# Moving one transposition ahead of its product, and the conversions around it, in a delta-rule attention with a gated MLP

## The chip, the cores and the metric

The kernel runs on one core of one Trainium2 chip. The metric is device microseconds of one execution. TensorE (PE) multiplies, VectorE (DVE) and ScalarE (ACT) do the elementwise work, GpSimd (POOL) clears a few buffers, SyncE (SP) issues the DMAs. Each engine runs its own list of instructions in order, and waits at an instruction until what it reads has been written and what it overwrites has been read.

## The reference

For each of 4 batches and 8 heads there is a recurrence over 768 tokens with a 48 x 48 state; its outputs, 3072 tokens of 384 numbers, go through a gated MLP of width 1536.

```python
k_n = k / (norm(k) + 1e-6)
for t in range(S):
    y[t] = q[t] @ state
    v_old = k_n[t] @ state
    state = state + beta[t] * outer(k_n[t], v[t] - v_old)
x = y.transpose(0, 2, 1, 3).reshape(B * S, H * D)
out = (sigmoid(x @ w_gate) * (x @ w_val)) @ w_out
```

## The kernel before

**Groups.** The tokens are cut into 12 groups of 64 per sequence (N = 12). Within a group the recurrence is solved as a triangular system: `gram` forms the products of keys (`G`, `L`), `norms` the key norms from them, a solver the inverse of the unit triangular matrix in blocks of 32, `rest`, `updates` and `rows` apply it to V and to the state, `advance` brings the state to the next group, and `flip` transposes the result into the MLP's input. Groups 0, 1 and 2 use `solve_halves`: it inverts 16-wide halves on DVE in `H`, copies them into `X` (L397), transposes `X` into `mt` (L400), and then joins the halves. The joining takes a product `pz` of `mt` with a lower-left block (L407, on PE), a second transposition `D` of `mt` on DVE (L420), a copy `Z` of `pz` on ACT (L421; `D` and `Z` lie in the tile `scratch`), a second product `pm` of both (L407), and the subtraction of `pm` from `mt` (L428). Groups 3 to 11 use `solve`, which has no joining.

**The MLP.** For each group the MLP runs in 12 pieces f of the hidden width: `gate_val` (PE, tile `gv`), `gated` (sigmoid on ACT at L564, product on DVE at L565, tile `sg`) and `outp` (PE, tile `po`) two pieces later. Group 0 multiplies full fp32 weights `u` (L556, L584); groups 1 to 11 multiply weights and inputs split into a high and a low part (`w`, L559, L590), the split on ACT (L212, high part) and DVE (L219, low part).

**Weights.** 36 pieces are loaded as 64-bit words (`raw`). ACT converts each piece in two instructions (`scaled`, L189 and L191), and the end of the conversion of piece n releases the load of piece n + 6. DVE joins the two words of a piece (L203, `u`). Later each `u` is split.

**Order.** The order on every engine is written by hand: `plan`, `late` and `tail` hold, for each slot s, steps that are issued in that slot. A slot pair issues one `gate_val` and one `outp`; `plan[s]` comes before the gating work of the slot, `late[s]` behind it, `tail[s]` last. Generators (`halves1`, `splits`, `scalings`) are advanced by the count that stands in the tables, from one `yield` to the next. So the place of a `yield` decides what is issued together. In `solve_halves` the transposition L400 and the product `pz` stand between the same two `yield`s, so for group 1 both are issued in slot 10, and for group 2 in slot 29.

`scale_v` multiplies V of a group by the key norms, 16 small ACT instructions (L279); `R`, the difference of V and `pk` (L455), needs it. PSUM tiles come from pools of two buffers; `pz` and `pm` take the two `aux` buffers that the key products of group 2 (`pg_2`) used before, and `pp_1` (keys by queries, L319) takes them next.

Of the kernel before, what the change touches and what calls it, by code (L numbers as in the profile page):

```python
# [55 lines left out]
def deltanet_gated_mlp(ctx: ExitStack, tc: tile.TileContext, kd, qd, kv, beta, words, out):  # L56
# [106 lines left out]
    pieces = [(0, "g"), (0, "v")]  # L163
# [20 lines left out]
    def scaled(n):  # L184

        half, lo, hi = words_of(n)
        nc.scalar.activation(lo.bitcast(I32), half, AF.Copy, bias=-4095.5 / 8192, scale=1 / 8192)  # L189
        h = hi.bitcast(F32)  # L190
        done[n] = nc.scalar.activation(h, h, AF.Prelu, scale=2.0 ** -112, alpha=-2.0 ** 32)  # L191
        if n + BEHIND in range(EAGER, len(pieces)):
            load_piece(n + BEHIND, done[n])
# [27 lines left out]
    def joining():  # L221
        for n in range(len(pieces)):
            join(n)
            yield

    def splitting():
        for n in range(len(pieces) + 1):
            if n:
                weight_lo(n - 1)
            if n < len(pieces):  # L230
                weight_hi(n)
            yield
# [43 lines left out]
    def scale_v(g):  # L276
        V, mq = state[g]["kv"][:, 1], state[g]["mq"]
        for c in range(CP):
            nc.scalar.activation(V[:, c], V[:, c], AF.Copy, scale=mq[:, c, 0:1])  # L279
            yield  # L280
# [92 lines left out]
    def solve_halves(g):  # L373
# [14 lines left out]
        for j in range(15, 0, -1):  # L388
            k, n = j // 2, 8 - j // 2
# [8 lines left out]
            yield  # L398
        A, D, Z = (joints[g][:, i] for i in range(3))
        nc.vector.transpose(mt.rearrange("q c (k r) -> q k c r", r=2), X.rearrange("q k (c r) -> q k c r", r=2))  # L400
        pool, tag = (ps_aux, "aux") if g else (ps_gv, "gv")
        pz, pm = (pool.tile([128, CP, 32], F32, name=f"{n}_{g}", tag=tag) for n in ("pz", "pm"))

# [199 lines left out]
    plan = collections.defaultdict(list)  # L603
    late = collections.defaultdict(list)

    def steps(gen, n=1):
        def fn():
            for _ in range(n):
                next(gen, None)
        return fn  # L610

    def spread(gen, total, lo, hi, room=lambda s: 1.0, into=plan):

        done, upto, whole = 0, 0.0, sum(room(s) for s in range(lo, hi))
        for s in range(lo, hi):
            upto += total * room(s) / whole
            n = total if s == hi - 1 else round(upto)
            into[s].append(steps(gen, n - done))
            done = n

    def chain(*gens):
        for q in gens:
            yield from q

    def take(gen, n=1):
        for _ in range(n):
            next(gen, None)

    def scaling(g, s):
        for i in range(4):  # L630
            plan[s + i].append(steps(scalings[g], 4))

    scalings = [scale_v(g) for g in range(N)]
    NORMS, SOLVE, HALVES = 18, 66, 40
    joins, splits = joining(), splitting()
# [27 lines left out]
    take(gram(1), 10)  # L663
    take(scale_v(0), CP)
    halves0, norms1, halves1 = solve_halves(0), norms(1), solve_halves(1)
    take(halves0, 38)
    for n in range(2, 6):
        scaled(n)
    take(norms1, 11)
# [28 lines left out]
    flip(0, 1)  # L698
    busy_array(gap[0], 2)
    tail = collections.defaultdict(list)  # L700
    for n, at in enumerate((0, 0, 0, 1, 2, 2, 4, 5, 6, 8, 9, 10, 11, 12, 12, 13, 14, 15, 16, 16, 17, 18, 18), 13):
        plan[at].append(lambda n=n: scaled(n))
    spread(joins, len(pieces) - 4, 0, 20)
    for at, n in ((0, 8), (1, 4), (2, 6), (3, 4), (4, 5), (5, 5), (9, 1), (10, 1), (11, 1)):
        plan[at].append(steps(halves1, n))
    plan[10].append(steps(halves1))
    spread(splits, 12, 9, 24, into=tail)
    spread(splits, len(pieces) + 1 - 12, 24, 44, into=tail)
    for s in (7, 8):
        plan[s].append(steps(scalings[1], 8))  # L710
    for part in (1, 0):
        plan[6].append(lambda part=part: load_rows(2, part))
    plan[8].append(lambda: load_q(2))
    halves2 = solve_halves(2)
    plan[12].append(lambda: clear(2))
    plan[23].append(lambda: joint(2))
    plan[24].append(lambda: lower_left(2))

    busy = collections.Counter()
# [18 lines left out]
    for g in range(N):  # L738
# [20 lines left out]
        else:  # L759
# [4 lines left out]
            if g > 2:  # L764
                solves.append((g, w - 13 if g == 3 else w - 14, w + 9))
            scaling(g, {2: 25, 3: 43}.get(g, w - 7))
    spread(chain(norms(2), halves2), NORMS + 36, 8, 27, lambda s: max(0.1, 1.6 - busy[s]))
    for at in (29, 30, 30, 31):
        plan[at].append(steps(halves2))
    for g, lo, hi in solves:  # L770
        spread(chain(norms(g), solve(g)), NORMS + SOLVE, lo, hi, lambda s: max(0.1, 1.6 - busy[s]))
# [72 lines left out]
```

## Time and profile before

| what | value |
|---|---|
| time, median of 3 runs | 651.9 us (651.75 to 652.64) |
| the profiled execution's own time | 652.21 us |
| its span, first to last instruction | 650.5 us |
| mean granted TensorE clock | 0.991 |
| PE busy | 626.4 us (96%) |
| DVE busy | 467.9 us (72%) |
| ACT busy | 321.2 us (49%) |

The profiled execution takes 1.7 us around its span and stands 0.3 us above the median. Times in the text are microseconds from the start of the span. In a list of instructions by time, the first number is the start, the second the time until the end of the (merged) instructions of that row, "x" their count, and in brackets the idle time of the engine ahead of them and what ended it. In the table by stretches each engine's busy time is followed by its number of instructions; PEclk is the granted TensorE clock as a share of full speed.

### The profile page before, as it was taken

How to read it: one execution, taken by the hardware profiler on the slowest of the kernel's cores; microseconds unless marked ns; L12 is line 12 of the kernel's file. 1: busy time of each engine (PE TensorE's matmuls, PEld its weight loads, DVE VectorE, ACT ScalarE, POOL GpSimd, SP SyncE). 2: the span in 40 equal slices, each digit the busy share in tenths (PEclk: the TensorE clock that was granted, in tenths of full speed). 3: DMA queues.
4: the chain of work that ended last, by engine and by line, in shares of the span. 5: the costliest groups of instructions: out<-in, count | busy, mean ns of one | idle time of the engine just before them, and what ended most of it. 6: DMA issues, size and time to landing. Idle time of an engine off the chain costs nothing.

```text
span 650.5 us, 24072 instructions
## 1 busy us (share of the span) xinstructions
PE 626.4 (96%) x10556; PEld 585.0 (90%) x10556; DVE 467.9 (72%) x1443; ACT 321.2 (49%) x870; POOL 11.3 (2%) x30
## 2 busy tenths in 40 slices
PE   6788999799999999999999999999999999999996
PEld 4466778789999999999999999999999999999996
DVE  5887687568887977977967977977977977952221
ACT  5889385566455355355355355355355355334221
POOL 5000000000000000000000000000000000000000
PEclk9999799899999999999999999999999999999999
DMA  9597422201212103112102012113112100100101
GB/s 256 193 323 249 131 75 84 51 4 32 77 28 85 25 28 85 25 28 84 25 28 85 20 33 84 26 28 85 25 28 84 25 4 3 25 3 3 25 1 25
DMA packets 17769, 41.07 MB, mean 63 GB/s; under 512 B 4224, under 2 KB 7296, under 8 KB 17664
## 3 DMA queue, kind: packets, MB, share of 16 engines
q1 hardware_dynamic: 17664, 39.53, 21.1%
q8 instruction: 83, 1.36, 0.9%
q14 instruction: 22, 0.18, 0.1%
HBM read 34.80 MB, written 4.72 MB: 61 GB/s over the span
## 4 chain that ended last, share of the span: by engine, by line
PE 89%; DVE 5%; ACT 3%; issue 1%; DMA 1%; ACTq 0%; SPq 0%; DVEq 0%
PE gv L559 43%; PE po L590 22%; PE gv L556 4%; PE pu L475 3%; PE pg L291 2%; PE yy L501 2%; PE yy L504 2%; PE pp L319 2%; PE po L584 2%; PE pd L522 2%; PE pk L444 1%; PE pk L467 1%; PE pt L540 1%; ACT kv L279 1%; DVE kqp L324 1%
## 5 line engine op out<-in xcount | busy, mean ns | idle before, releaser
L559 PE MATMUL gv<-xx,w 128*128 128x256 f32 x2376 | 308.5, 284 | 0.0
L559 PEld LDWEIGHTS gv<-xx,w 128*128 128x128 f32 x2376 | 302.3, 191 | 0.9
L590 PE MATMUL po<-w,h 128*128 128x384 f32 x792 | 166.5, 345 | 0.0
L564 ACT ACTIVATE sg<-gv 128x256 f32<-128x256 f32 x144 | 55.3, 384 | 203.4 <-PE gv L559 190.6
L590 PEld LDWEIGHTS po<-w,h 128*128 128x128 f32 x792 | 133.3, 188 | 3.4 <-issue 0.3
L565 DVE TENSOR_TENSOR sg<-sg,gv 128x256 f32<-128x256 f32 x144 | 60.4, 419 | 85.2 <-ACT sg L564 84.7
L570 ACT CAST h<-sg 128x256 fp32r<-128x256 f32 x132 | 53.5, 405 | 53.0 <-DVE sg L565 51.6
L350 DVE TENSOR_TENSOR X<-X,tmp 128x126 f32<-128x126 f32 (+22 forms) x279 | 71.3, 256 | 8.9
L347 DVE TENSOR_TENSOR tmp<-X,gp 128x126 f32<-128x126 f32 (+22 forms) x279 | 71.0, 254 | 7.9
L575 DVE TENSOR_TENSOR h<-sg,h 128x256 fp32r<-128x256 f32 x132 | 55.1, 417 | 29.8 <-ACT h L570 29.8
L481 ACT COPY su<-pu 32x384 f32<-32x384 f32 x92 | 43.3, 471 | 15.2 <-PE pu L475 14.0
L279 ACT ACTIVATE kv<-kv,mq 128x48 f32<-128x48 f32 x192 | 48.1, 329 | 0.0
L556 PE MATMUL gv<-xx,u 128*128 128x256 f32 x144 | 35.8, 402 | 0.3 <-DVE xx L543 0.3
L529 DVE TENSOR_TENSOR su<-su,pd 48x384 f32<-48x384 f32 x40 | 22.1, 552 | 18.9 <-PE pd L522 18.4
L324 DVE TENSOR_TENSOR kqp<-pp,pmask 64x512 f32<-64x512 f32 x48 | 32.3, 687 | 3.4 <-PE pp L319 2.4
L303 ACT COPY G<-pg 32x256 f32<-32x256 f32 (+1 forms) x69 | 25.4, 368 | 18.6 <-PE pg L291 17.4
L556 PEld LDWEIGHTS gv<-xx,u 128*128 128x128 f32 x144 | 28.2, 201 | 5.5 <-ACT xx L543 0.8
L455 DVE TENSOR_TENSOR R<-kv,pk 128x384 f32<-128x384 f32 x44 | 22.4, 550 | 1.5 <-PE pk L444 1.5
L212 ACT CAST w<-u 128x384 fp32r<-128x384 f32 x36 | 18.2, 508 | 6.2 <-DVE w L219 5.9
L475 PEld LDWEIGHTS pu<-R,mt 32*32 32x32 f32 x1408 | 16.5, 105 | 4.9 <-issue 1.7
L219 DVE TENSOR_TENSOR w<-u,w 128x384 fp32r<-128x384 f32 x36 | 19.4, 550 | 1.5 <-ACT w L212 1.4
L475 PE MATMUL pu<-R,mt 32*32 32x48 f32 x1408 | 19.4, 202 | 0.9 <-DVE kqp L324 0.9
(104 smaller groups left out, 518.3 us busy)
## 6 DMA issues: line engine op xcount, KB each, us to landing
raw<-in_words_dram SPq DMA_DIRECT2D x36, 384.0 KB, 5.0
kv<-in_kv_dram SPq DMA_DIRECT2D x24, 384.0 KB, 5.0
kqp<-in_qd_dram SPq DMA_DIRECT2D x24, 256.0 KB, 4.2
kqp<-in_kd_dram SPq DMA_DIRECT2D x24, 192.0 KB, 3.6
out_dram<-ot SPq DMA_DIRECT2D x48, 96.0 KB, 2.2
beta<-in_beta_dram SPq DMA_DIRECT2D x12, 16.0 KB, 4.5
```

Of the source, the lines that this page charges most:

```text
L279: nc.scalar.activation(V[:, c], V[:, c], AF.Copy, scale=mq[:, c, 0:1])
L347: nc.vector.tensor_tensor(out=tmp, in0=X[:, k:16, j:j + 1].to_broadcast([128, n, j]), in1=gp[:, j:j + 1, 0:j].to_broadcast([128, n, j]), o ...
L350: nc.vector.tensor_tensor(out=X[:, k:16, 0:j], in0=X[:, k:16, 0:j], in1=tmp, op=ALU.add)
L475: nc.tensor.matmul(out=pu[0 if g else x][r:r + 32, j], lhsT=mt[r:r + 32, e * J + j], rhs=R[e][r:r + 32, j], start=True, stop=True)
L481: nc.scalar.copy(su[r:r + 32, 3 if x else e], pu[0][r:r + 32])
L556: nc.tensor.matmul(out=pg[:, o], lhsT=parts[w, f][:, k * 128:(k + 1) * 128], rhs=x[0][:, k], start=k == 0, stop=k == KC - 1)
L559: nc.tensor.matmul(out=pg[:, o], lhsT=parts[w, f][:, a, k * 128:(k + 1) * 128], rhs=x[b][:, k], start=(k == 0 and q == 0), stop=(k == KC - ...
L564: nc.scalar.activation(h, st["gv", f][:, 0], AF.Sigmoid)
L565: nc.vector.tensor_tensor(out=h, in0=h, in1=st["gv", f][:, 1], op=ALU.mult)
L570: nc.scalar.copy(hh[:, 0], st["sg", f])
L575: nc.vector.tensor_tensor(out=hh[:, 1], in0=st["sg", f], in1=hh[:, 0].bitcast(F32), op=ALU.subtract)
L590: nc.tensor.matmul(out=po[s], lhsT=hh[:, a, ts], rhs=parts["o", f][:, w], start=(f == 0 and q == 0), stop=(f == NF - 1 and q == 2))
```

## The change

A `yield` now stands between the transposition L400 and the product `pz`, so the tables can issue the transposition in an earlier slot than the product. The other edits follow from that or go with it:

- `take(halves0, 39)`: group 0 takes one step more, since it has one `yield` more; its order is the same as before.
- Group 1: the transposition is issued in slot 6 (the added `(6, 1)`), the product stays in slot 10.
- Group 2: the steps of norms and halves are spread over slots 8 to 24 instead of 8 to 26, the transposition is issued in slot 26, the product stays in slot 29.
- Conversions of pieces 15 to 23 (`scaled`) are issued up to three slots later; piece 24 and those behind it stay, and so do 13 and 14.
- V of group 1 is scaled four instructions at a time at the end of slots 4 to 7, instead of eight at a time within slots 7 and 8.
- Splits of weights 12 to 30: three steps in slots 24 to 28, the others in slots 29 to 43; before, 25 steps were spread evenly over 24 to 43.

```diff
         A, D, Z = (joints[g][:, i] for i in range(3))
         nc.vector.transpose(mt.rearrange("q c (k r) -> q k c r", r=2), X.rearrange("q k (c r) -> q k c r", r=2))
+        yield
         pool, tag = (ps_aux, "aux") if g else (ps_gv, "gv")
...
-    take(halves0, 38)
+    take(halves0, 39)
...
-    for n, at in enumerate((0, 0, 0, 1, 2, 2, 4, 5, 6, 8, 9, 10, 11, 12, 12, 13, 14, 15, 16, 16, 17, 18, 18), 13):
+    for n, at in enumerate((0, 0, 1, 2, 3, 5, 6, 8, 9, 9, 10, 10, 11, 12, 12, 13, 14, 15, 16, 16, 17, 18, 18), 13):
         plan[at].append(lambda n=n: scaled(n))
     spread(joins, len(pieces) - 4, 0, 20)
-    for at, n in ((0, 8), (1, 4), (2, 6), (3, 4), (4, 5), (5, 5), (9, 1), (10, 1), (11, 1)):
+    for at, n in ((0, 8), (1, 4), (2, 6), (3, 4), (4, 5), (5, 5), (6, 1), (9, 1), (10, 1), (11, 1)):
         plan[at].append(steps(halves1, n))
     plan[10].append(steps(halves1))
     spread(splits, 12, 9, 24, into=tail)
-    spread(splits, len(pieces) + 1 - 12, 24, 44, into=tail)
-    for s in (7, 8):
-        plan[s].append(steps(scalings[1], 8))
+    spread(splits, 3, 24, 29, into=tail)
+    spread(splits, len(pieces) + 1 - 15, 29, 44, into=tail)
+    for s in range(4, 8):
+        tail[s].append(steps(scalings[1], 4))
...
-    spread(chain(norms(2), halves2), NORMS + 36, 8, 27, lambda s: max(0.1, 1.6 - busy[s]))
-    for at in (29, 30, 30, 31):
+    spread(chain(norms(2), halves2), NORMS + 36, 8, 25, lambda s: max(0.1, 1.6 - busy[s]))
+    for at in (26, 29, 30, 30, 31):
         plan[at].append(steps(halves2))
```

Lines behind the new `yield` are one higher in the changed kernel, and two higher from the loop over `scalings` on. The lists of PE and POOL are the same in both kernels. What moves stands on DVE, ACT and SP, at these places.

**DVE, group 1.** The list of DVE before, from the last join ahead of the sigmoid product of piece 3 (`u_7` from `raw_14`) to the transposition into `mt`:

```order
L203 SCALAR_TENSOR_TENSOR u_7_1013<-raw_14_620 128x384
L565 TENSOR_TENSOR sg_0_3_1024<-sg_0_3_1024,gv_0_3_1002 128x256
L203 SCALAR_TENSOR_TENSOR u_7_1013<-raw_15_716 128x384
L203 SCALAR_TENSOR_TENSOR u_8_1030<-raw_16_720 128x384
L203 SCALAR_TENSOR_TENSOR u_8_1030<-raw_17_772 128x384
L240 STREAM_TRANSPOSE gp_2_1062<-G_2_918 128x1024
L565 TENSOR_TENSOR sg_0_4_1064<-sg_0_4_1064,gv_0_4_1040 128x256
L455 TENSOR_TENSOR R_1_0_1101<-kv_1_113,pk_1_0_1067 128x384
L455 TENSOR_TENSOR R_1_1_1102<-kv_1_113,pk_1_1_1068 128x384
L203 SCALAR_TENSOR_TENSOR u_9_1111<-raw_18_776 128x384
L203 SCALAR_TENSOR_TENSOR u_9_1111<-raw_19_803 128x384
L400 STREAM_TRANSPOSE mt_78<-X_1_559 128x16x16x2
```

and in the changed kernel:

```order
L397 COPY X_1_559<-H_1_725 128x8x16 x2
L203 SCALAR_TENSOR_TENSOR u_7_1013<-raw_14_620 128x384
L400 STREAM_TRANSPOSE mt_78<-X_1_559 128x16x16x2
L566 TENSOR_TENSOR sg_0_3_1025<-sg_0_3_1025,gv_0_3_1002 128x256
L203 SCALAR_TENSOR_TENSOR u_7_1013<-raw_15_716 128x384
L203 SCALAR_TENSOR_TENSOR u_8_1035<-raw_16_720 128x384
L203 SCALAR_TENSOR_TENSOR u_8_1035<-raw_17_772 128x384
L240 STREAM_TRANSPOSE gp_2_1055<-G_2_914 128x1024
```

The transposition goes ahead of ten instructions; the others keep their order among themselves, and behind the joins of `u_9` follow at once the small instructions of `norms(2)`, the joins of `u_10` and the transposition `D`, as before.

**ACT, group 1.** The list of ACT before, from the sigmoid of piece 2 on (`raw` rows are conversions, `kv_1` the scaling of V, `G_2` and `L_2` copies of key products of group 2):

```order
L564 ACTIVATE sg_0_2_980<-gv_0_2_954 128x256
L189 ACTIVATE raw_20_807<-raw_20_807 128x384
L191 ACTIVATE raw_20_807<-raw_20_807 128x384
L303 COPY G_2_918<-pg_2_1_921 32x32x8 x2
L189 ACTIVATE raw_21_811<-raw_21_811 128x384
L191 ACTIVATE raw_21_811<-raw_21_811 128x384
L308 COPY L_2_919<-pg_2_0_920 32x256 x2
L308 COPY L_2_919<-pg_2_1_921 32x256 x2
L564 ACTIVATE sg_0_3_1024<-gv_0_3_1002 128x256
L279 ACTIVATE kv_1_113<-kv_1_113,mq_1_669 128x48 x8
L189 ACTIVATE raw_22_833<-raw_22_833 128x384
L191 ACTIVATE raw_22_833<-raw_22_833 128x384
```

and in the changed kernel:

```order
L565 ACTIVATE sg_0_2_972<-gv_0_2_950 128x256
L279 ACTIVATE kv_1_113<-kv_1_113,mq_1_669 128x48 x4
L189 ACTIVATE raw_18_776<-raw_18_776 128x384
L191 ACTIVATE raw_18_776<-raw_18_776 128x384
L303 COPY G_2_914<-pg_2_1_917 32x32x8 x2
L279 ACTIVATE kv_1_113<-kv_1_113,mq_1_669 128x48 x4
L189 ACTIVATE raw_19_803<-raw_19_803 128x384
L191 ACTIVATE raw_19_803<-raw_19_803 128x384
L308 COPY L_2_915<-pg_2_0_916 32x256 x2
L308 COPY L_2_915<-pg_2_1_917 32x256 x2
L565 ACTIVATE sg_0_3_1025<-gv_0_3_1002 128x256
L279 ACTIVATE kv_1_113<-kv_1_113,mq_1_669 128x48 x8
```

Before, the other eight scalings and then the sigmoid of piece 4 follow, then pieces 23, 24 and the copy `Z` (one weight split between). In the changed kernel there follow piece 20, the sigmoid of piece 4, then pieces 21 to 24 and the copy `Z`. Ahead of the sigmoid of piece 4 stand pieces up to 22 before, up to 20 now; the conversion of piece 18 was already ahead of the copies of the state (L527), and 19 behind them.

**DVE, group 2.** The list of DVE before, from the low part of the first hidden piece of group 1 (`h_1_0`) to the transposition:

```order
L575 TENSOR_TENSOR h_1_0_1798<-sg_1_0_1786,h_1_0_1798 128x256
L565 TENSOR_TENSOR sg_1_1_1866<-sg_1_1_1866,gv_1_1_1839 128x256
L219 TENSOR_TENSOR w_13_1837<-u_6_991,w_13_1837 128x384
L219 TENSOR_TENSOR w_14_1870<-u_7_1013,w_14_1870 128x384
L219 TENSOR_TENSOR w_15_1873<-u_7_1013,w_15_1873 128x384
L575 TENSOR_TENSOR h_1_1_1889<-sg_1_1_1866,h_1_1_1889 128x256
L565 TENSOR_TENSOR sg_1_2_1918<-sg_1_2_1918,gv_1_2_1894 128x256
L455 TENSOR_TENSOR R_2_0_1955<-kv_2_1015,pk_2_0_1921 128x384
L455 TENSOR_TENSOR R_2_1_1956<-kv_2_1015,pk_2_1_1922 128x384
L219 TENSOR_TENSOR w_16_1892<-u_8_1030,w_16_1892 128x384
L400 STREAM_TRANSPOSE mt_78<-X_2_1349 128x16x16x2
```

and in the changed kernel:

```order
L324 TENSOR_TENSOR kqp0_76<-pp_2_1_1802,pmask_81 64x512 x2
L400 STREAM_TRANSPOSE mt_78<-X_2_1349 128x16x16x2
L576 TENSOR_TENSOR h_1_0_1799<-sg_1_0_1787,h_1_0_1799 128x256
L566 TENSOR_TENSOR sg_1_1_1864<-sg_1_1_1864,gv_1_1_1837 128x256
L219 TENSOR_TENSOR w_12_1791<-u_6_987,w_12_1791 128x384
L576 TENSOR_TENSOR h_1_1_1884<-sg_1_1_1864,h_1_1_1884 128x256
L566 TENSOR_TENSOR sg_1_2_1910<-sg_1_2_1910,gv_1_2_1886 128x256
L456 TENSOR_TENSOR R_2_0_1947<-kv_2_1016,pk_2_0_1913 128x384
L456 TENSOR_TENSOR R_2_1_1948<-kv_2_1016,pk_2_1_1914 128x384
L219 TENSOR_TENSOR w_13_1868<-u_6_987,w_13_1868 128x384
L219 TENSOR_TENSOR w_14_1952<-u_7_1013,w_14_1952 128x384
L421 STREAM_TRANSPOSE scratch_2_1750<-mt_78 128x512
```

The transposition goes ahead of ten instructions, and three weight splits fewer stand ahead of `R_2` (12 is the last there, 15 before) and four fewer ahead of `D` (14 is the last, 18 before). On ACT the high parts of the same weights move back likewise: ahead of the sigmoid of `sg_1_2` 13 is the last now, 16 before. On SP the load of V and K rows of group 2 and one query load now stand ahead of the loads of pieces 26 to 28, which follow their conversions.

## The prediction

> **What bounds the kernel now.** I read the table by stretches first, to see where PE stops and where its clock drops; then the waits; then the chain of waits through the two stops. Columns of the table: stretch and length, then busy time of PE, weight loads, DVE, ACT and POOL, then PEclk, DMA share and GB/s.
>
> ```profile
> core 0: us, PE busy (x) PEld busy (x) DVE busy (x) ACT busy (x) POOL busy (x), PEclk, DMA share, GB/s
> 35.22:38.63 3.41, 2.19 (x65) 1.19 (x52) 2.33 (x8) 1.63 (x5) 0.00 (x0) 1.00 1.02 350
> ...
> 62.52:65.93 3.41, 0.70 (x3) 0.08 (x1) 2.46 (x6) 3.11 (x9) 0.00 (x0) 1.00 1.02 279
> 65.93:69.34 3.41, 2.81 (x130) 2.66 (x131) 3.27 (x10) 0.59 (x1) 0.52 (x1) 0.50 0.67 219
> 69.34:72.75 3.41, 3.41 (x9) 2.70 (x8) 0.68 (x4) 0.00 (x0) 0.00 (x0) 0.50 0.02 5
> ...
> 120.54:123.95 3.41, 0.38 (x44) 0.41 (x46) 2.96 (x7) 1.68 (x6) 0.00 (x0) 1.00 0.64 155
> 123.95:127.36 3.41, 3.41 (x116) 3.35 (x104) 1.31 (x3) 1.05 (x2) 0.00 (x0) 0.50 0.02 5
> ...
> 130.00:640.00 510.00, 508.84 (x8300) 496.23 (x8300) 370.55 (x1157) 231.18 (x643) 0.00 (x0) 1.00 0.14 36
> ```
>
> From 130 us on PE works 508.84 of 510 us, so what PE gains earlier comes out at the end, and nothing there can be gained by order. Before, there are two holes, and behind each the granted clock is 0.50: for 6.8 us behind the first, for 3.4 us behind the second. Who ends the holes:
>
> ```profile
> PE pz L407 <- DVE mt L400: 3.4, 1, 3.4
> PE pz L407 <- DVE n L244: 3.3, 1, 3.3
> ...
> PE pu L475 <- DVE kqp L324: 0.9, 1, 0.9
> ```
>
> Both large ones are the product `pz`. The second row names L244, the instruction right behind the transposition L400 on DVE; in the chain it is L400 itself that ends just ahead of `pz`:
>
> ```profile
> 65.76 0.62 DVE mt L400
> 66.53 1.93 PE pz L407 x128
> 68.46 4.93 PE gv L556 x12
> 73.39 1.22 PE pm L407 x82
> 76.09 1.09 PE pp L319 x64
> 77.18 2.79 PE gv L556 x12
> ...
> 123.58 1.75 PE pz L407 x81
> 125.33 3.27 PE gv L559 x18
> 128.60 1.22 PE pm L407 x82
> 131.07 2.16 PE gv L559 x18
> ```
>
> The same 12 matmuls of `gv` take 4.93 us behind the first hole and 2.79 us at 77.18; the same 18 take 3.27 us behind the second and 2.16 us at 131.07. PE was done with its last product ahead of the holes at these times (start plus length: 63.22 and 120.21; the first row ends the product that a sigmoid is to read below, at 52.90):
>
> ```profile
> 50.04 2.86 PE L556 MATMUL gv<-xx,u 128*128 128x256 f32 x12
> ...
> 61.66 1.56 PE L584 MATMUL po<-u,sg 128*128 128x384 f32 x4
> ...
> 118.89 1.32 PE L590 MATMUL po<-w,h 128*128 128x384 f32 x6
> ```
>
> **The change part by part.** PE's list does not change, so the question is only what each of its waits finds.
>
> *Group 1, the transposition.* `X` is complete well ahead of both holes (the join `u_7` behind its copies and the transposition now stand in front of the sigmoid product of piece 3), and the two PSUM buffers are read out by the copies of `pg_2` ahead of the sigmoid of piece 3, at 58.30 before. So `pz` follows its neighbour at 63.22, 3.31 us earlier, and takes 1.22 us (the row of `pm`, as many matmuls at full clock) in place of 1.93; the `gv` behind it takes 2.79 in place of 4.93. PE then stands before `pm` at 63.22 + 1.22 + 2.79 = 67.23, where it stood at 73.39.
>
> *What is late next: `D` and `Z`.* `pm` needs the transposition `D` on DVE and the copy `Z` on ACT. Both stand behind the sigmoid of piece 4 (ACT) and its product (DVE). The rows of ACT and DVE around them:
>
> ```profile
> 53.68 0.39 ACT L564 ACTIVATE sg<-gv 128x256 f32<-128x256 f32 x1
> 58.30 0.38 ACT L564 ACTIVATE sg<-gv 128x256 f32<-128x256 f32 x1
> 60.38 0.55 ACT L189 ACTIVATE raw<-raw 128x384 int32<-128x384 uint16 x1
> 61.28 1.90 ACT L279 ACTIVATE kv<-kv,mq 128x48 f32<-128x48 f32 x8
> 63.08 0.36 ACT L564 ACTIVATE sg<-gv 128x256 f32<-128x256 f32 x1
> 68.52 0.59 ACT L421 COPY scratch<-pz 128x512 f32<-128x512 f32 x1 [2.89 <-PE pz L407]
> ```
>
> ```profile
> 59.05 1.49 DVE L203 SCALAR_TENSOR_TENSOR u<-raw 128x384 uint32<-128x384 uint32 x3
> 60.46 1.24 DVE L240 STREAM_TRANSPOSE gp<-G 128x1024 f32<-128x1024 f32 x1
> 63.48 0.42 DVE L565 TENSOR_TENSOR sg<-sg,gv 128x256 f32<-128x256 f32 x1 [1.78 <-ACT sg L564]
> 68.62 0.71 DVE L420 STREAM_TRANSPOSE scratch<-mt 128x512 f32<-128x512 f32 x1
> 69.91 0.21 DVE L255 TENSOR_TENSOR ns<-ny,gp 128x32 f32<-128x32 f32 x1
> 73.84 0.42 DVE L565 TENSOR_TENSOR sg<-sg,gv 128x256 f32<-128x256 f32 x1 [3.72 <-ACT sg L564]
> 75.11 0.68 DVE L428 TENSOR_TENSOR mt<-mt,pm 128x512 f32<-128x512 f32 x1
> ```
>
> A conversion costs 61.28 - 60.38 = 0.90 us of ACT, eight scalings 63.08 - 61.28 = 1.80. The sigmoid of piece 2 could start 0.90 earlier than 53.68 without piece 19 ahead of it, but its product ends at 52.90, so it gains 0.7. To the sigmoid of piece 4 the count is three conversions in place of four with the same sixteen scalings: 0.90 earlier less those 0.2, so 62.4 in place of 63.08. The sigmoid of piece 3 has one conversion fewer and eight scalings more ahead of it: 58.30 - 0.90 + 1.80 + 0.2 = 59.4. On DVE its product, three joins (1.41 us, 59.05 to 60.46) and the transposition `gp` (1.24) then end near 62.8, when the sigmoid of piece 4 is done too (62.4 + 0.36). So the product at 63.48 moves to 62.8, and all behind it by 0.7 us, `D` by 0.62 more for the transposition that is gone: start 68.62 - 1.3 = 67.3, end 68.0. Then `pm` starts near 68.15 (with the 0.14 us that lay between L400's end and `pz`). `Z` is not later: from 62.4 a sigmoid, four conversions and a split are about 4.3 us, then 0.59 for `Z`: 67.3. So a hole of about 0.9 us opens before `pm`, and `pm` is 73.39 - 68.15 = 5.2 us earlier. Bounds: if the sigmoid of piece 4 does not get earlier at all, `D` ends at 68.7 and the hole is 1.6; if DVE and ACT are ready, it is 0.
>
> *The step behind it.* `pp` takes the buffer of `pm` and waits for the subtraction L428. From the start of `D` to that of the subtraction DVE now has, without a wait between, 1.50 us to the end of L255, one small instruction of some 0.2 that is moved ahead, and 1.27 us (73.84 to 75.11): 67.3 + 3.0 = 70.3, end 71.0, so `pp` near 71.1. PE comes there 2.70 us behind the start of `pm` (76.09 - 73.39): 70.85. Loss 0.25. With the 1.09 us of `pp` the next `gv` starts near 72.2 in place of 77.18: **group 1 gains 5.0 us** (bounds 4.3 to 6.2).
>
> *Loads.* A conversion's end releases the load six pieces on:
>
> ```profile
> raw<-in_words_dram SPq DMA_DIRECT2D x36, 384.0 KB, 5.0
> ```
>
> Piece 18 is converted near 55 now, so piece 24 lands near 60 and is wanted near 65.5. Piece 20, near 62.2, releases 26, which lands near 67.5 behind the loads that now stand ahead of it on SP; ACT comes to it only behind `Z`, a sigmoid, a split and piece 25, near 69. Cost 0; if it were late, ACT has no sigmoid to give until `gv` at 72.2 ends, 2.79 us on.
>
> *Group 2.* `mt` is written behind the masks of `pp_2`, ten instructions earlier, so `pz` follows at 120.21, 3.37 us earlier, and takes 1.22 in place of 1.75; `gv` takes 2.16 in place of 3.27. PE is before `pm` at 123.6, before at 128.60. `D` again:
>
> ```profile
> 123.35 0.99 DVE L219 TENSOR_TENSOR w<-u,w 128x384 fp32r<-128x384 f32 x2
> ...
> 124.25 0.71 DVE L420 STREAM_TRANSPOSE scratch<-mt 128x512 f32<-128x512 f32 x1
> ```
>
> Without L400 (0.62) and with one split fewer between `R` and `D` (0.45, half of 124.25 - 123.35) it ends at 123.9 even if `R` is not earlier: a hole of 0.4 at most. Ahead of `R` three splits fewer stand on DVE, and on ACT three high parts fewer ahead of the sigmoid that `R` waits behind. I take 0: **group 2 gains 5.0 us** (4.5 to 5.0).
>
> *Splits later.* Nothing on PE asks for them in the holes; from slot 43 on the lists agree again. They lie under PE's 508.84 busy us. Their worst is in the rivals. The wait of 0.9 us on L324 stays: as many instructions stand ahead of it.
>
> *Sum.* 652.2 (the profiled execution: span 650.5 and 1.7 around it) - 5.0 - 5.0 = 642.2. That execution is 0.3 above the median of 651.9, so the forecast is **641.9**.
>
> The clock's part of the sum goes by the two matmul groups behind each hole: 0.71 + 2.14 + 0.53 + 1.11 = 4.5 us. The Trainium skill (TensorE: Matmul & The Clock Gate, "Terms") prices a throttle as its time times (1 - K/N): 10.2 us at half clock would be 5.1. By that the forecast would be 641.3; the row from 65.93 shows why it is less here, 0.60 of those us were idle anyway.
>
> **The rivals.**
>
> *The stop moves to `pm`.* If the sigmoid of piece 4 and `R` do not come earlier and DVE loses the 0.62 too (`D` ends at 69.33 as before), `pm` starts at 69.5 behind a hole of 2.2 us, and one stretch at half clock costs 1.7: group 1 gains 73.39 - 69.5 - 1.7 = 2.2, in all 7.2: 644.7. For it: DVE was busy 3.27 of 3.41 us from 65.93. Against it: the lists take work away ahead of `D`.
>
> *Short holes hold the clock down.* Holes of 0.9 and 0.25 us lie a few us apart; if two stretches stay at 0.50, that is half of 6.8 us: 645.3. Against it: from 35.22 PE is busy 2.19 of 3.41 us at clock 1.00, less than any stretch of group 1 would be (3.41 - 0.9 = 2.5). The Trainium skill (TensorE: Matmul & The Clock Gate, "A second HAM failure mode: psum-queue depth-cycling") says that frequent micro-idles between groups of matmuls make the clock swing between half and full. By that rule this rival is the outcome; the row from 35.22 speaks against it.
>
> *Nothing changes.* If `pz` waits for something that ends with L400 by chance, the time stays 651.9. The chain against it: `mt` ends at 66.38, `pz` starts 0.14 later.
>
> *Slower: piece 24 lands late.* Its conversion stands ahead of `Z` on ACT, and its load is released some 6 us later than before. From a landing at 66.2 on (`Z` then ends at 68) each us goes to `pm` one for one; to lose the whole 10.0 it would land 10 us behind that, 21 us after its release, against 5.0 in the row. A landing at 78.2 would give 654.
>
> **How the numbers follow.** Forecast 641.9: 0.74, with its own range 640.7 (gains of 6.2 and 5.0) to 643.1 (4.3 and 4.5). Stop at `pm` 644.7: 0.11. Short holes 645.3: 0.07. Nothing changes 651.9: 0.05. Slower 654: 0.03. Range 639.8 to 646.2: below, the wait of 0.9 us on L324 might go too (640.7 - 0.9); above, it takes in the two rivals that keep a gain, with 0.9 to spare. It leaves out about a tenth; two tenths with what I may have overlooked. What a measurement of this kernel tells from no change is about 0.2%, 1.3 us: faster 0.92, same 0.05, slower 0.03.
>
> **What would show it.** Right: no wait of `pz` on L400; clock 1.00 in all stretches from 62 to 130 us; the first `gv` behind `pz` 2.8 us long; a wait before `pm` on L420 (now L421) of 0.5 to 1.6 us and a short one before `pp`; DVE's product of piece 4 near 62.8. Wrong: a row at 0.50, a wait of over 2 us before `pm`, a `gv` that waits for a join or a split, or PE idle behind 130 us that was not there.

## The result and the profile after

| | before | changed |
|---|---|---|
| time, median | 652.0 us (651.75 to 652.64, 5 runs) | 649.05 us (646.76 to 649.93, 5 runs) |
| ratio, 95% interval | | 0.9941 [0.9922, 0.9961] |
| profiled execution, its span | 652.21, 650.5 | 646.87, 645.2 |
| mean granted TensorE clock of it | 0.991 | 0.994 |

The ratios in this document leave out one slow execution, 848.18 us at a granted clock of 0.658, of the version "transposition alone" below (its median is 646.20 without it). The change gains 3 us where 10 were forecast, and 649.05 lies outside the range. Both old stops are gone, and a new one stands in their place. PE in group 1 of the changed kernel, by time (start, length, instruction, in brackets the idle time ahead and what ended it):

```profile
62.68 1.56 PE L585 MATMUL po<-u,sg 128*128 128x384 f32 x4
64.17 1.47 PE L408 MATMUL pz<-mt,scratch 32*32 32x32 f32 x128
65.57 2.86 PE L557 MATMUL gv<-xx,u 128*128 128x256 f32 x12
68.73 0.31 PE L408 MATMUL pm<-scratch 32*32 32x32 f32 x12 [0.30 <-DVE nt L249]
69.59 1.19 PE L408 MATMUL pm<-scratch 32*32 32x32 f32 x116 [0.55 <-issue]
70.71 1.56 PE L585 MATMUL po<-u,sg 128*128 128x384 f32 x4
72.20 0.34 PE L319 MATMUL pp<-kqp 48*64 48x64 f32 x7
75.45 1.08 PE L319 MATMUL pp<-kqp 48*64 48x64 f32 x57 [2.92 <-issue]
76.47 2.86 PE L557 MATMUL gv<-xx,u 128*128 128x256 f32 x12
```

`pz` follows `po` at once, `gv` behind it runs at full clock, `pm` waits 0.30 us for `D` (the view names L249, the instruction right behind `D` on DVE; `D` ends at 68.58, `pm` starts at 68.73). Then PE stops twice in the middle of a product, 0.55 us in `pm` and 2.92 in `pp`. "issue" says that the profile shows nothing that PE waited for: the matmuls behind both stops read and write what those just ahead of them did. The waits of PE up to 135 us, and group 2:

```profile
PE pp L319 <- issue: 2.9, 1, 2.9
PE pu L476 <- issue: 2.5, 2, 1.5
PE pm L408 <- issue: 0.8, 2, 0.6
```

```profile
119.49 1.29 PE L408 MATMUL pz<-mt,scratch 32*32 32x32 f32 x128
120.70 2.41 PE L560 MATMUL gv<-xx,w 128*128 128x256 f32 x18
123.05 0.54 PE L408 MATMUL pm<-scratch 32*32 32x32 f32 x39
123.86 0.96 PE L408 MATMUL pm<-scratch 32*32 32x32 f32 x89 [0.28 <-issue]
```

Group 2 went as forecast but for 0.28 us of the same kind. The table by stretches, first of before, then of the changed kernel (last three columns PEclk, DMA share, GB/s):

```profile
70.00:72.00 2.00, 2.00 (x7) 1.55 (x6) 0.12 (x1) 0.00 (x0) 0.00 (x0) 0.50 0.00 0
72.00:74.00 2.00, 2.00 (x85) 1.52 (x85) 0.16 (x1) 0.58 (x2) 0.00 (x0) 0.81 0.04 8
```

```profile
70.00:72.00 2.00, 2.00 (x95) 1.35 (x84) 1.51 (x3) 1.83 (x5) 0.00 (x0) 1.00 1.03 397
72.00:74.00 2.00, 0.54 (x8) 0.20 (x7) 0.00 (x0) 0.22 (x1) 0.00 (x0) 1.00 1.03 387
...
130.00:640.00 510.00, 508.80 (x8244) 496.33 (x8242) 370.34 (x1158) 231.25 (x644) 0.00 (x0) 1.00 0.14 36
```

The DMA was idle in this stretch before (share 0.00 and 0.04) and is full now (1.03). Behind 130 us nothing has changed. So the question of the experiments is what PE misses at 72.54 us, and whether the full DMA has to do with it.

Beside the data queue q1 the profile has queues of the kind "instruction"; the larger one is q8. Over the whole span of the changed kernel, then from 69.6 to 73.0 us, then from 73.0 to 74.2 (packets, MB, share of the 16 engines):

```profile
q8 instruction: 83, 1.36, 0.9%
```

```profile
q1 hardware_dynamic: 478, 1.30, 102.6%
```

```profile
q1 hardware_dynamic: 164, 0.44, 95.7%
q8 instruction: 1, 0.02, 5.7%
```

1.36 MB in 83 packets are 16.4 KB each; PE has 21,104 recorded instructions (10,548 matmuls and 10,556 weight loads), 254 per packet, 255 with its 99 semaphore and drain instructions. Counted in all of these the stops in `pm` and `pp` lie at numbers 2233 and 2489, exactly 256 apart. In the profile of "extra loads" below, which has all of PE's matmuls, the four stops of the first 80 us marked "issue" in `pu`, `pm` and `pp` have 962, 1218, 2242 and 2498 such records ahead of them: every distance is a multiple of 256. The packet of q8 that ends ahead of the second one starts at 73.01 and ends at 74.10; PE goes on at 75.45. In the 3.4 us before, there is none.

**Theory A.** PE's instructions come in blocks of 256. When PE passes a border between two blocks, the next block but one is asked for. With seven weight loads on the queues the packet starts 3.42 us after the border (69.59 to 73.01) instead of about 1.1, and PE has used up what it had. **Theory B:** `pz`, `pm` and `pp`, small matmuls of some 10 ns each (1.29 us for 128 of `pz`), use blocks faster than any fetch brings them, whatever the DMA does. **Theory C:** no fetch; `pp` waits for something of its own that the profile does not name.

The Trainium skill (Runtime: NRT & Kernel Launch, "Instruction fetch mechanics") describes such a fetch: blocks of 16 KiB or 256 instructions, brought by a DMA queue that the sequencer drives while it runs the block before, the crossing "mostly hidden". The size agrees with the rows; whether it is hidden is what the runs decide.

### The profile page after: what moved, and what is told of

It is laid out like the page before. It is cut to its first block, busy times and chain, and to the rows that moved or that the text cites. A ratio compares the mean times of both kernels' runs of the same rounds, so it can differ in the third digit from the quotient of the medians.

```text
span 645.2 us, 24064 instructions
## 1 busy us (share of the span) xinstructions
PE 622.1 (96%) x10548; PEld 582.1 (90%) x10556; DVE 467.3 (72%) x1443; ACT 320.6 (50%) x870; POOL 11.3 (2%) x30
## 3 DMA queue, kind: packets, MB, share of 16 engines
q8 instruction: 83, 1.36, 0.9%
## 4 chain that ended last, share of the span: by engine, by line
PE 91%; DVE 4%; ACT 2%; issue 2%; DMA 1%; ACTq 0%; SPq 0%; DVEq 0%
PE gv L560 44%; PE po L591 23%; PE gv L557 3%; PE pu L476 3%; PE yy L502 2%; PE yy L505 2%; PE po L585 2%; PE pg L291 2%; PE pp L319 2%; PE pk L445 2%; PE pd L523 2%; PE pk L468 1%; PE pt L541 1%; PE pm L408 1%; PE pz L99 1%
## 5 line engine op out<-in xcount | busy, mean ns | idle before, releaser
L324 DVE TENSOR_TENSOR kqp<-pp,pmask 64x512 f32<-64x512 f32 x48 | 32.2, 686 | 7.3 <-PE pp L319 6.3
L557 PE MATMUL gv<-xx,u 128*128 128x256 f32 x144 | 33.7, 385 | 0.3 <-ACT xx L544 0.3
L557 PEld LDWEIGHTS gv<-xx,u 128*128 128x128 f32 x144 | 26.6, 190 | 4.9 <-ACT xx L544 0.8
L189 ACT ACTIVATE raw<-raw 128x384 int32<-128x384 uint16 x36 | 19.9, 553 | 0.2 <-DMA raw<-in_words_dram 0.2
```

The source lines that it names most:

```text
L557: nc.tensor.matmul(out=pg[:, o], lhsT=parts[w, f][:, k * 128:(k + 1) * 128], rhs=x[0][:, k], start=k == 0, stop=k == KC - 1)
```

## The experiments

All edits are against the changed kernel where nothing else is said; each ratio is to executions of the kernel before in the same series. The table collects the profiles: start of the first `gv` of group 0 (end of the start-up), from there to the `gv` behind `pp_1` (group 1), and from there to the end of the span (group 2 and the rest). By the prediction's steps the last two columns would be 29.2 (77.11 - 42.88 - 5.0) and 568.4 (650.5 - 77.11 - 5.0). (77.11 is the start of that `gv` in the list by time, as in the other rows; the chain in the prediction has 77.18, the end of `pp` ahead of it.)

| kernel | median us | ratio to before, 95% | first `gv` | group 1 | rest |
|---|---|---|---|---|---|
| before | 652.0 | | 42.88 | 34.23 | 573.4 |
| changed | 649.05 | 0.9941 [0.9922, 0.9961] | 43.90 | 32.57 | 568.7 |
| changed, again | 648.12 | 0.9921 [0.9898, 0.9944] | 44.13 | 33.10 | 570.7 |
| loads early | 645.63 | 0.9888 [0.9868, 0.9908] | 43.20 | 32.39 | 568.8 |
| gap in the loads | 643.31 | 0.9873 [0.9845, 0.9900] | 46.95 | 29.55 | 568.1 |
| gap, again | 643.81 | 0.9868 [0.9848, 0.9887] | 42.68 | 30.04 | 568.7 |
| gap and start | 642.26 | 0.9843 [0.9823, 0.9863] | 41.69 | 29.55 | 568.4 |
| extra loads in group 2 | 650.39 | 0.9990 [0.9967, 1.0013] | 42.04 | 32.46 | 572.2 |
| borders shifted | 648.38 | 0.9938 [0.9916, 0.9960] | 42.21 | 34.36 | 569.9 |
| transposition alone | 646.26 | 0.9898 [0.9875, 0.9921] | 42.61 | 31.05 | 569.7 |
| transposition alone, gap | 645.01 | 0.9890 [0.9867, 0.9912] | 42.85 | 30.84 | 569.8 |
| lists alone | 650.52 | 0.9971 [0.9948, 0.9993] | 44.58 | 34.20 | 569.9 |

**1. The loads earlier.** The releases of the loads stand in a table; no instruction of PE, DVE or ACT changes its place.

```diff
-        if n + BEHIND in range(EAGER, len(pieces)):
-            load_piece(n + BEHIND, done[n])
+        for m in RELEASE.get(n, ()):
+            load_piece(m, done[n])
...
-    EAGER, BEHIND = 14, 6
+    RELEASE = {n: [n + 6] for n in range(8, 17)}
+    RELEASE.update({17: [23, 24, 25, 26], 18: [27, 28, 29, 30], 19: [31, 32, 33], 28: [34], 29: [35]})
```

> The changed kernel with nothing moved but the release of the weight loads 24 to 35: pieces 23 to 26 behind the conversion of piece 17, 27 to 30 behind 18, 31 to 33 behind 19, 34 and 35 behind 28 and 29, so that few data packets should be on the DMA queues from 68 to 74 us (all instructions of PE, DVE and ACT keep their order). Theory A (the 2.92 us inside the second pp are PE's next block of 256 instructions, whose fetch started 3.42 us after it was asked for because seven weight loads stood on the queues): the hole in pp falls to 0.6 us or less (1.1 us from request to packet and 2.4 more to the next matmul, as where the DMA is idle, against the 3.0 us of matmuls that PE has in hand), the 0.55 inside pm shrinks or goes, and the median comes to 646.1 or less (649.05 - 2.9). Theory B (pz, pm and pp take their blocks faster than any fetch brings them, loads or not): 2.9 us of hole stays, 649.

```profile
68.07 0.31 PE L408 MATMUL pm<-scratch 32*32 32x32 f32 x12 [0.52 <-DVE nt L249]
70.39 1.65 PE L408 MATMUL pm<-scratch 32*32 32x32 f32 x116 [2.01 <-issue]
71.98 2.59 PE L585 MATMUL po<-u,sg 128*128 128x384 f32 x4
74.50 1.16 PE L319 MATMUL pp<-kqp 48*64 48x64 f32 x64
```

The hole in `pp` is gone: `pp` runs through in 1.16 us. The full stretch of the DMA has moved ahead, to 62 to 68 us (share 1.02 to 1.07), and the stop has moved with it, to the border before: 2.01 us inside `pm` instead of 0.55, with a stretch at half clock behind it. That the 0.55 would shrink was wrong, since the loads had not gone but moved. The block of `pp` was asked for at 70.39 with an empty DMA, and its packet started at 71.50, 1.11 us later. This supports A, and B alone cannot be it: the order of PE's list is the same, and the stop followed the loads. But PE's pace has a part in the hole that is gone: at half clock PE took some 4.2 us from the border in `pm` to the one in `pp` (70.39 to 74.6), 2.95 in the changed kernel (69.59 to 72.54), so the block had more time. Experiment 4 shows the same border without a half clock.

**2. Loads where there were none.** Six loads are added ahead of `pm_2`.

```diff
...
+    def extra_loads():
+        for i in range(6):
+            t = spare.tile([128, 2 * PW], U32, name=f"extra_{i}", tag=f"extra_{i}", bufs=1)
+            nc.sync.dma_start(t, words[i])
+    plan[28].append(extra_loads)
```

> The changed kernel with six extra loads of 384 KB each (weight words copied to spare DRAM that nothing reads), issued near 117 to 121 us, so that the DMA queues are full when pz_2 asks for the block of pm_2. Nothing else is changed. Theory A: the packet that started 1.3 us behind the start of pz_2 comes 2.5 to 4 us behind it, and the 0.28 us of issue inside pm_2 become 1.5 to 3; with one more stretch at 0.50 perhaps: 650.5 to 653. Theory B (order and pace of PE alone): 0.28 stays and the time is that of the change, 649.

```profile
122.92 0.54 PE L409 MATMUL pm<-scratch 32*32 32x32 f32 x39
124.86 0.96 PE L409 MATMUL pm<-scratch 32*32 32x32 f32 x89 [1.40 <-issue]
```

The stop after the 39th matmul of `pm_2` grows from 0.28 to 1.40 us, a little under the 1.5 expected; the packet starts 3.5 us behind the start of `pz_2` (119.21 to 122.69), where it had been 1.7 (119.49 to 121.22; the 1.3 of the expectation is too low). So loads alone make such a stop. Group 1, which this edit leaves alone, has the stop in `pp` once more, 2.92 us. The time (650.39) lies just below what A expected; its spread (648.3 to 655.8) is too wide to weigh 1.1 us by it.

**3. The borders shifted by half a block.** 64 tiny matmuls ahead of `pz` of group 0:

```diff
             paced = beats[8::2]
+            for i in range(64):
+                nc.tensor.matmul(out=pz.rearrange("q a b -> q (a b)")[:, 0:16], lhsT=flat[:, 0:128], rhs=flat[:, 0:16], start=True, stop=True)
```

> The changed kernel with 64 small extra matmuls (128 instructions of PE with their weight loads, writing into pz of group 0 before its real product) where PE waits for the halves of group 0 near 13 us. They shift every later border of 256 instructions by half a block against the program. Theory A and B (instruction blocks): the 2.92 us inside pp at its ninth matmul are gone from there; the borders now lie inside pz and inside pm (after some 76 of its 128 matmuls), a stop stands there and a smaller one in the gv behind pp; in sum 0.5 to 2 us instead of 3.5, 647 to 648.5. Theory C (pp waits for something of its own, a buffer or an operand that the profile does not name): 2.9 us before the same ninth matmul of pp, 649.

```profile
64.81 0.54 PE L408 MATMUL pz<-mt,scratch 32*32 32x32 f32 x40 [0.96 <-issue]
...
68.07 0.85 PE L408 MATMUL pm<-scratch 32*32 32x32 f32 x76
71.87 0.80 PE L408 MATMUL pm<-scratch 32*32 32x32 f32 x52 [2.94 <-issue]
...
75.45 1.19 PE L319 MATMUL pp<-kqp 48*64 48x64 f32 x64
```

The stops moved by half a block, to the matmul that was named (76 of `pm` ahead of it); `pp` has none. C is out: it is a place in PE's instruction stream, not an operand. The size was not foreseen: 0.96 + 2.94 us, because the packet asked for at 64.81 started only at 69.35, 4.54 us later. Where the borders lie is no cure while the loads stay.

**4. A gap in the loads.** Pieces 24 to 28 are released earlier, the V and K rows of group 2 are issued two slots earlier, and pieces 29 to 33 with the queries of group 2 only behind the masks of `pp_1`:

```diff
...
+    RELEASE = {n: [n + 6] for n in range(8, 17)}
+    RELEASE.update({17: [23, 24, 25, 26, 27], 18: [28], 28: [34], 29: [35]})
...
-        plan[6].append(lambda part=part: load_rows(2, part))
-    plan[8].append(lambda: load_q(2))
+        plan[4].append(lambda part=part: load_rows(2, part))
...
+            late[11].append(lambda: (load_q(2, state[1]["cut"]), stage(29, 34, state[1]["cut"])))
```

(`state[1]["cut"]` is the last mask instruction at L324.)

> The changed kernel with a gap in the loads: pieces 24 to 27 behind the conversion of piece 17 and 28 behind 18 (landed near 60 us), V, K and beta of group 2 issued two slots earlier, and q of group 2 and pieces 29 to 33 only behind the last mask of pp_1 (near 75 us). Nothing but loads should differ. Theory A (data packets on the queues delay PE's next block): with an idle DMA from 63 to 75 us the packet starts 1.1 us after it is asked for at both borders, so no issue hole inside pm (loads early: 2.01 us), one of at most 1 us inside pp (the change: 2.92), and no stretch at clock 0.50 behind them. Against loads early pp starts 3 us earlier: 642 to 643.5 in the median. If the holes in pm and pp came from the order of PE alone, 2 to 3 us would stand in one of them here too: 645 or more.

> The changed kernel with the gap in the loads, again: its first six executions lay at 641.5 to 642.0 (three) and 644.6 to 646.5 (three), and the profiled one of these had lost 3.8 us before the first gv (46.95 us where others have 42.0 to 43.9). Theory: what differs between its executions lies ahead of the first gv; behind it the time to the end of the span is 597.5 to 598.5 us in each profile, 10 us less than before (607.6). Median 642 to 644.

The second repeats the first in another series; these are its lines:

```profile
67.55 1.40 PE L408 MATMUL pm<-scratch 32*32 32x32 f32 x128 [0.52 <-DVE nt L249]
...
70.37 0.34 PE L319 MATMUL pp<-kqp 48*64 48x64 f32 x7
71.70 1.08 PE L319 MATMUL pp<-kqp 48*64 48x64 f32 x57 [1.00 <-issue]
72.72 2.86 PE L557 MATMUL gv<-xx,u 128*128 128x256 f32 x12
```

No stop in `pm`, 0.45 (first profile) and 1.00 us (second) in `pp`, the clock at 1.00 through both. The stretches of `pm` and `pp` in the first profile, where `pm` starts at 71.80 and the 57 matmuls of `pp` at 75.49 (last three columns PEclk, DMA share, GB/s):

```profile
72.00:74.00 2.00, 2.00 (x130) 1.60 (x120) 1.93 (x7) 2.00 (x6) 0.00 (x0) 1.00 0.03 8
74.00:76.00 2.00, 1.55 (x42) 0.87 (x44) 0.54 (x1) 0.80 (x2) 0.00 (x0) 1.00 0.00 0
```

The DMA is idle there, so what is left of the stop is B's part: PE's own pace. The loads account for the rest, 3.47 us of stops (0.55 and 2.92) less 0.45 to 1.00. Medians 643.31 and 643.81, as expected of A, 4 to 6 us below the changed kernel. Group 1 is at 29.55 and 30.04 where the prediction's steps give 29.2. The first series still had 46.95 us of start-up in its profile; the time behind the first `gv` (597.7 and 598.7, the second a little above what was expected) differs by 1 us where the start-up differs by 4.3.

**5. The parts.** The transposition alone (against the kernel before: the `yield`, `take(halves0, 39)`, `(6, 1)` and the two lines of group 2), the same with the gap of experiment 4, and the other half alone (conversions, splits and scalings of the change, the transposition back beside `pz`).

> The kernel before with the transposition alone issued ahead (group 1 and group 2); conversions, splits and V's scaling in the order of before. Conversions then release the loads as before (pieces 28 to 30 had landed by 69.35 us there). Theory A: pz follows at 63 us, a hole before pm of 0.9 to 2.2 us, since the sigmoid of piece 4 is not earlier, but none above 1 us inside pp; group 1 gains 2 to 4 us, group 2 its 4 to 5: 644 to 646.5, better than the whole change. Theory B: a hole of about 2.9 us inside pp here too: 648 to 649.

> The transposition alone ahead (conversions, splits and V's scaling in the order of before), with the same gap in the loads. Theory A: the 0.97 us inside pp shrink to 0.5 or so; the holes before pm that wait for D (1.58 us in group 1, 1.06 in group 2) stay, since DVE's and ACT's lists are the same: 645 to 646. The difference to the changed kernel with the gap is then what the lists are worth once the fetches are out of the way: 2 to 3 us.

> The other half: conversions, splits and V's scaling in the order of the change, the transposition back beside pz. pz waits for the transposition again and the clock falls behind the hole, so PE asks for its blocks later and takes them at half speed. Theory A and B alike: holes at both pz of 2.5 to 3.4 us as before, 650.5 to 653; if it came out below 650, the lists and not the transposition would carry part of the 3 us that the change gained.

The transposition alone makes 646.26, and the whole change, with more edits, 648 to 649: by the medians the lists cost 2 to 3 us as long as the loads follow them. The stop in `pp` is 0.97 us there, not 2.92; pieces 27 to 30 had landed by 69.7 us:

```profile
72.64 1.08 PE L319 MATMUL pp<-kqp 48*64 48x64 f32 x57 [0.97 <-issue]
```

With the gap the order turns round: 645.01 against 643.3 to 643.8, so the lists are worth 1.2 to 1.7 us, less than the 2 to 3 expected. (The intervals of these ratios overlap; it is the rows of group 1 and the rest in the table that tell them apart.) They are what brings `D` earlier; without them, with the gap:

```profile
68.44 1.49 PE L408 MATMUL pm<-scratch 32*32 32x32 f32 x128 [1.23 <-DVE nt L249]
...
121.56 1.28 PE L408 MATMUL pm<-scratch 32*32 32x32 f32 x128 [1.06 <-DVE scratch L421]
```

against 0.52 and no wait with them. That the stop in `pp` would shrink to 0.5 there was a miss: it was 1.00 with an empty DMA. The lists alone gave 650.52: in group 1 `pz` still waits 2.52 us (it starts at 67.45, `mt` ends at 67.30), in group 2 only 1.05, less than the 2.5 expected.

**6. The changed kernel again.**

> The changed kernel as it is, beside the two with a gap, for a second profile. Theory A: 2.7 to 3.1 us inside pp of group 1 again, at the same matmul; in some executions one stretch at 0.50 behind it, which would make the difference between 646.9 and 649. Median 649, 5 to 6 us above the version with the gap.

```profile
75.44 1.86 PE L319 MATMUL pp<-kqp 48*64 48x64 f32 x57 [3.19 <-issue]
```

```profile
76.00:78.00 2.00, 2.00 (x51) 1.79 (x44) 0.72 (x2) 0.00 (x0) 0.00 (x0) 0.50 0.18 62
78.00:80.00 2.00, 2.00 (x7) 1.55 (x6) 1.97 (x4) 0.00 (x0) 0.00 (x0) 0.50 0.00 0
```

The stop is there again, at the same matmul, 3.19 us long (a little above the 2.7 to 3.1 named). In this execution the clock is at 0.50 behind it, so the 57 matmuls of `pp` take 1.86 us instead of 1.08 and the `gv` behind them is slow too; the first profile had 1.00 there. The two profiles differ by 2.7 us of span: 0.2 of start-up, 0.5 to the `gv` behind `pp_1`, and 2.0 behind that, most of it the clock. The median of 648.12 is 4.3 us above the gap's, less than the 5 to 6 expected.

**7. The same cure for the start-up.** On top of the gap, loads at 31 us are put off: q and K rows of group 1 to slot 2, pieces 12 and 13 and k of group 2 behind the conversion of piece 8.

```diff
...
-    load_q(1, state[0]["joint"])
...
-    stage(12, 14, lower_left(1))
-    load_rows(1, 0)
-    load_k(2)
+    lower_left(1)
     for n in range(6, 9):
         scaled(n)
+    load_k(2)
...
+    plan[2].append(lambda: (load_q(1), load_rows(1, 0)))
```

> The gap in the loads of group 1, and beside it fewer loads on the queues at 31 us, where two of three profiles with the gap or the change show PE before pu_0 (its 1217th recorded instruction) without its block for 0.7 to 2.6 us: q of group 1 and V-side rows of group 1 move to slot 2, pieces 12 and 13 and k of group 2 behind the conversion of piece 8. Theory A: the block asked for at 31 us comes after 1.1 to 2 us instead of 2.5 to 4.6, that stop falls to 0.5 us or less and the start-up (to the first gv) ends near 42 us in every execution: median 641 to 642.3, with a spread of 1.5 us or less (the gap alone: 643.3, 641.5 to 646.5). Rival: the stops before pu_0 come from PE's pace; start-up and spread as with the gap alone, 643.

(The expectation's "V-side rows" of group 1 are its K rows.)

```profile
34.58 0.88 PE L476 MATMUL pu<-kv,mt 32*32 32x48 f32 x62 [0.20 <-DVE kv L456]
...
66.53 1.49 PE L408 MATMUL pm<-scratch 32*32 32x32 f32 x128 [0.49 <-DVE nt L249]
...
70.23 1.08 PE L319 MATMUL pp<-kqp 48*64 48x64 f32 x57 [0.45 <-issue]
71.24 2.86 PE L557 MATMUL gv<-xx,u 128*128 128x256 f32 x12
```

The stop inside `pu` at the second border of the start-up, 1.22 us in the profile of before and 1.49 in that of the changed kernel, is gone; the one at the first border, 1.03 us, stays. 642.26 us, all of its runs between 641.5 and 642.7: the fastest of the versions, 10.2 us below the kernel before in the same series (652.43). Its parts are 29.55 and 568.4, and the start-up is 1.2 us shorter than before.

**The fetches side by side.** Behind a stop the time of passing the border is exact (PE stood there and went on). Eight of them, from the records of the instruction packets, times in us:

```
kernel, place                  border   next packet    later   PE goes on at the next border,
                               passed   from - to      by      behind the packet's end by
loads early, pm                70.39    71.50 - 72.94  1.11    no stop
gap and start, start-up        30.59    32.12 - 33.14  1.53    no stop
gap again, start-up            31.27    34.33 - 35.38  3.06    1.26
changed, pm                    69.59    73.01 - 74.10  3.42    1.35
extra loads, pm                67.63    71.16 - 72.25  3.53    1.24
changed again, start-up        31.08    35.37 - 36.58  4.29    1.51
borders shifted, pz            64.81    69.35 - 70.46  4.54    1.41
gap, start-up                  31.63    36.27 - 37.52  4.64    1.40
```

The packet itself takes 1.0 to 1.4 us in every row, and PE goes on 1.2 to 1.5 us behind its end. What varies is when it starts. In the row of 1.53 the share of the DMA falls from 0.90 to 0.08 at 32 us, when the packet starts.

These eight are a choice. The twelve profiles have 61 stops of at least 0.15 us marked "issue" (without the filler matmuls of helper L99), and in all of them PE goes on 1.1 to 1.6 us behind the end of an instruction packet. Where the DMA share from there to the next packet is below 0.1 (28 stops), that packet starts 1.04 to 1.67 us later; where it is 0.85 or more (29 stops), 1.40 to 7.24 us later, 3.42 at the median. So a full DMA makes a late packet likely, not certain. Four stops in `pp` with a share of 0.55 to 0.80 have 1.05 us, no more than on an idle DMA.

## Why the prediction was wrong, step by step

**The stops at `pz`, right.** `pz` follows its neighbour in both groups, and the `gv` behind it takes 2.86 and 2.41 us, not 4.93 and 3.27.

**What is late next, right.** The start-up of the profiled execution ended 1.02 us later than before (43.90 against 42.88), so 1.02 is taken off here. DVE in the changed kernel:

```profile
63.72 0.42 DVE L566 TENSOR_TENSOR sg<-sg,gv 128x256 f32<-128x256 f32 x1
...
67.88 0.70 DVE L421 STREAM_TRANSPOSE scratch<-mt 128x512 f32<-128x512 f32 x1
...
70.83 0.69 DVE L429 TENSOR_TENSOR mt<-mt,pm 128x512 f32<-128x512 f32 x1
76.56 0.69 DVE L324 TENSOR_TENSOR kqp<-pp,pmask 64x512 f32<-64x512 f32 x1 [5.04 <-PE pp L319]
```

The product of piece 4 comes at 62.7 (forecast 62.8), `D` at 66.9 (67.3), the subtraction at 69.8 (70.3). The hole before `pm` is 0.30 us where 0.9 was forecast, within the bounds of 0 to 1.6 though under the 0.5 that was named as a sign; `pp` did not wait for the subtraction. The wait of `pu_2` for L324 stayed, as said: in the last version

```profile
PE pu L476 <- DVE kqp L324: 0.9, 1, 0.9
```

**The loads, wrong: this is the step that failed.** "Cost 0; if it were late, ACT has no sigmoid to give until `gv`". They were asked for one thing only, whether ACT gets its data in time, and there it held (one wait of 0.17 us):

```profile
71.22 0.56 ACT L189 ACTIVATE raw<-raw 128x384 int32<-128x384 uint16 x1 [0.17 <-DMA raw<-in_words_dram]
```

```profile
raw<-in_words_dram SPq DMA_DIRECT2D x36, 384.0 KB, 5.6
```

But the later conversions release seven loads (pieces 27 to 33, issued 65.03 to 72.24, landed 71.20 to 77.94) right into the stretch in which PE runs `pz`, `pm` and `pp` without a hole. There PE stops for 2.92 us in `pp` and 0.55 in `pm`; with the loads out of the way 0.45 to 1.00 and nothing are left, so the loads that were put at 0 cost 2.5 to 3.0 us, and PE's own pace, for which the sum has no term, the rest. Behind it stood the sentence "PE's list does not change, so the question is only what each of its waits finds": PE also stops where no wait stands. In the kernel before, the stop at `pz`, the half clock and the idle DMA had given each block time to come.

The profile of before held the hint. One row of its waits, which I passed over, names no releaser; the second of its two stops, 1.22 us before 36.83, lies in the stretch from 35.22 that the prediction quotes with a DMA share of 1.02:

```profile
PE pu L475 <- issue: 2.3, 2, 1.2
```

**The sum.** Group 1: 5.0 forecast, 1.7 in the profile (34.23 - 32.57), 4.2 to 4.7 with the gap. Group 2: 5.0 forecast, 4.7 (573.4 - 568.7), and 4.7 to 5.3 with the gap. So the terms were right to within 0.8 us where the fetches are out of the way. (That the last version comes to 642.26 is no proof of 641.9, since its start-up is 1.2 us shorter than the sum had it.) From 641.9 to the 649.05 measured lead the two stops in group 1 (3.5), 1.0 to 1.25 us of start-up, up to 0.5 in group 2, and in some executions the stretch at half clock behind the stop, some 2 us more by the two profiles of the changed kernel. Those two stand at 646.87 and 649.61; no execution at the median itself was profiled.

**The rivals.** None was this one. "Slower: piece 24 lands late" looked at the right loads but at ACT's need of them. "The stop moves to `pm`" had the right form (a new stop where the old one went) and the wrong cause. "Short holes hold the clock down" did not come: with 0.49 and 0.45 us of idle time 4 us apart the profile of the last version shows a clock of 1.00. The rule of the Trainium skill quoted for that rival (TensorE: Matmul & The Clock Gate, "A second HAM failure mode: psum-queue depth-cycling") is not borne out by holes of this size. The clock did fall to 0.50 behind some of the stops of 2 to 3 us (2.01 in "loads early", 3.19 in the second profile of the changed kernel), but not behind the 2.92 in the first.

**The range and the chances.** Every case in them was made of waits, and no row of before had been asked what PE's instructions need; so the range ended at 646.2, and a slower outcome than that had 0.08 in all.

## What to carry to other kernels

When a change closes a stall, ask not only which wait ends last next, but what the stall had covered up: here the fetch of PE's own instructions, which starts late when data loads fill the DMA. Rows with "issue" in the waits of PE, in the middle of a group of equal matmuls, mark such places before a change; where runs of some hundred short matmuls follow each other, look at the DMA share in the 5 us ahead, and put the loads elsewhere. A release of loads that is tied to a moved instruction is part of the change, even if the data are in time.

## What the hardware showed that was not expected

- PE stops at borders of 256 instructions when the block is late: 0.18 to 3.19 us in the twelve profiles, with no wait named. From the border to the packet's start it takes 1.04 to 1.67 us on an idle DMA and 1.40 to 7.24 us on a full one; the packet takes 0.9 to 1.5 us, and PE goes on 1.1 to 1.6 us behind it. So by an estimate from these rows a block needs some 3.5 us even on an idle DMA (1.11 + 1.1 + 1.35), while `pm` uses one in some 1.3 us: the stop in `pp` stayed at 0.45 to 1.00 us even with an idle DMA. The Trainium skill (Runtime: NRT & Kernel Launch, "Instruction fetch mechanics") calls the crossing "mostly hidden"; here the measurement decides, and it is not.
- Whether the packet waits behind data descriptors on the DMA engines, or the request itself is held up, no run here separates.
- The start-up of one and the same order differs by up to 4 us from execution to execution (first `gv` at 42.68 and 46.95 us with the gap), of which the stop at the second border in `pu`, 0.67 and 2.59 us, makes 1.9. Another 2.0 lie behind that stop, where the clock is 0.50 from 38.15 to 44.98 us in the slower execution and 1.00 in the other.
